# A new order for the first 740 steps of a hand-ordered retention and SwiGLU kernel, and one more warm-up product

## The chip, the cores and the metric

The kernel runs on one core of a Trainium2 chip. The metric is the device time of one execution in microseconds (us). The core has a matrix engine (TensorE, in the profile PE, its weight loads PEld), three engines for elementwise work (VectorE or DVE, ScalarE or ACT, GpSimd or POOL), and SyncE (SP), whose queue issues nearly all transfers (DMA). Every engine runs its own instructions strictly in program order, and engines meet through semaphores. "On a queue" below always means in such an order.

## The reference

Two blocks in a row. The first is a recurrent retention over 4 batches, 8 heads, 768 positions, head size 64; the second a SwiGLU feed-forward block over the 3072 tokens with model size 512 and hidden size 1536.

```python
for t in range(S):
    state = gamma[None, :, None, None] * state + np.einsum('bhd,bhe->bhde', k[:, :, t], v[:, :, t])
    y[:, :, t] = scale * np.einsum('bhd,bhde->bhe', q[:, :, t], state)
...
x = np.ascontiguousarray(attn_out.transpose(0, 2, 1, 3)).reshape(B * S, H * D)
...
g = x @ w_gate
silu = g * (1.0 / (1.0 + np.exp(-g)))
val = x @ w_val
return (silu * val @ w_out).astype(np.float32)
```

The three weight matrices arrive in double precision and are converted in the kernel.

## The kernel before, in words

The tokens are cut into four segments. A segment is six chunks of 128 positions: three positions in each of two batches. For a chunk, retention is computed in blocks: scores (keys times queries, masked by a decay), their product with the values, the product of the queries with the carried state, and the update of the state. Then the segment goes through the feed-forward block: 12 blocks f of 128 hidden columns, gate and value products ("up"), the gating, and the product with w_out ("down") into six PSUM banks, one for each token block.

Matrix products work on fp32r operands. To keep accuracy, an operand is split into three parts (near_a and far_a on ACT, near_b and far_b on DVE, near_c or far_c on POOL or DVE) and a product is the sum over three parts. In the first segment the weights are loaded in double precision, converted by steps a, b, S, c, C on ACT, DVE and POOL, combined by T, split by n, used, and written to DRAM (Z) for the later segments.

There is no scheduler at run time. The order is written out by hand in the string PLAN: 2372 names of steps, and run() (in tile_retnet_swiglu) issues each step's instructions in that order. An instruction goes to the queue of its engine, so the plan fixes the order on each of the five queues at once; between engines only the semaphores of real dependencies hold. The same steps in another order compute the same values. The steps that the text names are these (f, n, p are numbers; a prefix such as 1/ is the segment, and none is the first part of segment 0):

- lN:W loads chunk N (W 0 keys, 1 queries, 2 values, 3 keys by rows); A0, A1, A2 load the table of decays; U, V load raw weights, Z keeps converted ones; P0, P1, P2 and 1/lN load chunks for segment 1; L loads two small vectors; all are issued by SP.
- rN transposes the keys of a chunk (lines 686), sN makes scores (646), mN mixes with the values (744), oN adds the old state (722), tN updates the state (707); kN and qN scale values and queries on POOL (663, 659), EN copies the rows.
- p, v are the up products of f = 0, 1 in three column parts (1080), G and W the gate and value products of f = 2 to 11 (1062), two each; i and u are SiLU on ACT, j and y the multiplication on DVE; g scales the state; h2 is a small preparation of tables for segment 1, M0 and M1 load its mask.
- 0/Wf loads a block of w_out into one of three split buffers, 0/df.0, .1, .2 split it, 0/Zf writes the split form to DRAM (so that 0/W of a later block waits until the 0/Z that reads the same buffer has landed); 0/hf.0, .1, .2 split the hidden values; 0/Df.b is the down product of block f for token block b (1306).
- 1/scp, 1/Ap, 1/Bp, 1/Cp are the matrix steps of segment 1's retention for p = 0, 1, 2 (830): scores, and three parts of the mixing. They need 1/decp (mask, DVE), 1/qp (scaled queries), 1/kp.i (scaled keys, mostly eight small ACT instructions each, line 973), 1/was (decayed state, ACT, 1031) and 1/new (added state, DVE, 1037). 1/y copies results out, 1/sum and 1/x build the operands of segment 1's up products, 1/p (1235), whose weights come by 1/Lf and 1/wf.

Before the plan starts, warm_up issues products of a zeroed tile with itself, ten of 128 columns and five of 16, on TensorE (line 1425; a product in this number format is two passes).

Of the kernel before, what the change touches and what calls it, by code (L numbers as in the profile page):

```python
# [25 lines left out]
L = 3  # L26
# [49 lines left out]
    1/y0.03 1/y0.05 0/d2.1 0/D1.5 1/y0.00 0/W3 0/D1.3 0/h2.1 1/y0.07 1/y0.12 1/y0.14 1/y0.13 1/l4  # L76
# [19 lines left out]
    1/w0.1.0 0/D11.4 1/sum2.2 0/Z11 1/x2.0.0 1/w0.0.2 1/w1.0.0 1/x2.1.1 1/x2.0.1 0/Z10 1/w1.0.1 0/e0
    0/o0 1/x2.0.2 1/w1.0.2 0/D11.5 1/p0.0 1/u0.0 1/p0.1 1/p0.2 1/p1.0 1/x2.2.0 1/u0.1 1/w0.2.0 0/e2
    0/o2 1/x2.2.1 1/w0.1.1 1/p1.1 1/w1.1.0 1/x2.2.2 1/u0.3 1/w1.2.0 1/u1.0 1/p1.2 1/u0.2 1/w0.2.1
    1/L3 1/w0.1.2 1/w1.2.1 1/w0.2.2 0/e1 1/p0.3 1/w2.2.0 1/w2.1.0 1/u0.4 0/e3 1/w1.1.1 1/w1.1.2 1/L4
    1/p0.4 1/u1.1 1/u0.5 1/p0.5 2/ta 1/w2.0.0 1/u0.6 1/u1.3 1/p0.6 1/p1.3 1/u1.4 1/u0.8 1/p1.4  # L100
# [18 lines left out]
    1/w10.0.2 1/p9.3 1/p9.2 1/u9.4 1/p8.6 1/u9.3 1/p9.4 1/p9.5 1/u8.2 1/u8.8 1/u8.9 1/p10.0 1/u9.5
    2/sc0 1/w9.2.2 1/u9.6 1/u9.1 1/p10.1 2/l5 2/l6 1/u8.7 1/w11.1.0 1/w11.0.0 1/w11.0.1 1/w11.1.1  # L120
    1/u10.0 1/w11.2.0 1/p10.2 1/p9.6 1/W0 2/l2 2/k0.1 1/u10.3 1/p10.3 1/u9.8 1/u9.9 1/p10.4 1/u10.4
    1/p10.5 1/h0.0 1/u10.1 2/dec0.0 1/u7.7 1/u9.2 1/u10.2 1/w10.2.1 1/u10.5 1/w11.1.2 1/w11.0.2
# [196 lines left out]
T0, UP0 = 30.0, 8.35  # L319
# [1188 lines left out]
```

## Time and profile before

| | us |
|---|---|
| timed runs | 637.96, 642.05, 643.54 |
| median of the three | 642.05 |
| the profiled execution | 638.92 |
| its span, first to last instruction | 637.1 |
| TensorE busy | 629.8 (99%) |
| VectorE busy | 509.1 (80%) |
| ScalarE busy | 394.9 (62%) |
| GpSimd busy | 178.2 (28%) |

The page divides the span into 40 slices and gives each engine's busy share in tenths; TensorE's row begins with an 8, ends with a 7, and has a 9 everywhere between. The chain that ended last is 94% TensorE and 3% DMA. TensorE's ends are modelled and its matrix products overlap in a pipeline, so that a product's mean duration in a row is longer than its distance to the next; distances are read from the chain of waits, which has no overlap. "Issue" is time in which an engine waited for nothing that the profile shows. A timeline row reads: start, duration, engine, line, operation, output and inputs, shape, count, and in brackets the idle time before it with what ended it. The granted clock of TensorE was 1.00 throughout.

### The profile page before, as it was taken

The page shows a single profiled execution, that of the slowest core. Times are in us where ns is not written, and L with a number is a line of the kernel's source. Part 1 is how long each engine was busy: PE and PEld are TensorE (multiplying, and loading weights), DVE is VectorE, ACT ScalarE, POOL GpSimd, SP SyncE. Part 2 cuts the span into 40 slices and gives each one's busy share as a digit, 9 for nine tenths or more (in the row PEclk, how much of TensorE's full clock was granted, in tenths as well). Part 3 has the DMA queues.
Part 4 walks back from the last instruction along what each step waited for, and adds up shares of the span by engine and source line. Part 5 has one row for each costly group of instructions (what it writes and reads, how often), then busy time and mean ns, then how long its engine had stood idle before and what let it go on. Part 6 is the DMA issues. An engine that isn't in the chain of part 4 may idle for free.

```text
span 637.1 us, 14140 instructions
## 1 busy us (share of the span) xinstructions
PE 629.8 (99%) x5607; PEld 581.2 (91%) x5607; DVE 509.1 (80%) x773; ACT 394.9 (62%) x836; POOL 178.2 (28%) x120
## 2 busy tenths in 40 slices
PE   8999999999999999999999999999999999999997
PEld 7999999978779999998788999998788999999886
DVE  6997898988989889977789677978878888877551
ACT  3787888677667665667477565656864655564220
POOL 3625555523532541120001343240002024232000
PEclk9999999999999999999999999999999999999999
DMA  8899998788876443687883436477785235303664
GB/s 314 280 350 345 344 359 291 289 309 309 295 268 232 162 164 119 191 272 222 276 320 120 155 109 223 158 228 217 237 303 198 102 135 190 133 17 133 231 214 149
DMA packets 58514, 142.82 MB, mean 224 GB/s; under 512 B 6864, under 2 KB 29264, under 8 KB 58448
## 3 DMA queue, kind: packets, MB, share of 16 engines
q1 hardware_dynamic: 57872, 141.14, 64.8%
q8 instruction: 44, 0.72, 0.5%
q10 hardware_dynamic: 576, 0.79, 0.3%
q14 instruction: 22, 0.18, 0.1%
HBM read 112.02 MB, written 29.88 MB: 223 GB/s over the span
## 4 chain that ended last, share of the span: by engine, by line
PE 94%; DMA 3%; DVE 1%; POOL 1%; issue 0%; ACT 0%; SPq 0%; DVEq 0%; POOLq 0%
PE bank L1235 41%; PE bank L1306 29%; PE bank L1062 13%; PE bank L830 5%; PE bank L1080 3%; DMA loads<-wup 1%; DMA hT<-in_q_t_dram 1%; DMA oitem<-wdnt 1%; PE bank L646 1%; DMA hT<-in_k_t_dram 1%; PE bank L744 1%; PE bank L722 1%; PE bank L707 0%; POOL gitem L1140 0%; POOL hT L659 0%
## 5 line engine op out<-in xcount | busy, mean ns | idle before, releaser
L1306 PE MATMUL bank<-oitem,gitem 128*128 128x512 f32 (+1 forms) x873 | 204.2, 391 | 0.5 <-DMA oitem<-wdnt 0.5
L1306 PEld LDWEIGHTS bank<-oitem,gitem 128*128 128x128 f32 x873 | 160.9, 188 | 34.8 <-DMA oitem<-wdnt 1.2
L1235 PE MATMUL bank<-xa,gitem 128*128 128x384 f32 x864 | 160.9, 335 | 0.0
L1235 PEld LDWEIGHTS bank<-xa,gitem 128*128 128x128 f32 x864 | 150.6, 188 | 0.4 <-DVE xa L1150 0.2
L1140 POOL TENSOR_TENSOR gitem<-gitem 128x768 fp32r<-128x768 f32 x36 | 72.4, 2014 | 185.0 <-DVE gitem L1137 160.2
L1140 POOL TENSOR_TENSOR oitem<-oitem 128x512 fp32r<-128x512 f32 (+1 forms) x48 | 53.6, 1124 | 157.6 <-DVE oitem L1137 125.7
L411 DVE SCALAR_TENSOR_TENSOR gitem<-gitem 128x768 fp32r<-128x768 f32 x84 | 86.0, 1033 | 1.3
L1235 PE MATMUL bank<-xb,gitem 128*128 128x384 f32 x432 | 84.0, 335 | 0.4 <-POOL gitem L1140 0.4
L1062 PE MATMUL bank<-xa,oitem 128*128 128x384 f32 x480 | 84.2, 335 | 0.0
L1062 PEld LDWEIGHTS bank<-xa,oitem 128*128 128x128 f32 x480 | 83.0, 188 | 0.3
L1235 PEld LDWEIGHTS bank<-xb,gitem 128*128 128x128 f32 x432 | 75.8, 188 | 1.1 <-POOL gitem L1140 0.7
L1134 ACT ACTIVATE gitem<-loads 128x768 fp32r<-128x768 f32 x72 | 59.1, 842 | 24.8 <-PE bank L1235 15.4
L1137 DVE SCALAR_TENSOR_TENSOR gitem<-gitem,loads 128x768 fp32r<-128x768 f32 x72 | 70.6, 993 | 3.4 <-ACT gitem L1134 3.3
L1134 ACT ACTIVATE gitem<-hT 128x768 fp32r<-128x768 f32 x48 | 40.1, 844 | 43.6 <-PE bank L1306 34.1
L1137 DVE SCALAR_TENSOR_TENSOR gitem<-gitem,hT 128x768 fp32r<-128x768 f32 x48 | 46.5, 978 | 22.5 <-ACT gitem L1134 18.6
L1235 PE MATMUL bank<-xb,oitem 128*128 128x384 f32 x216 | 43.0, 335 | 0.0
L1235 PEld LDWEIGHTS bank<-xb,oitem 128*128 128x128 f32 x216 | 38.0, 188 | 0.0
L1251 ACT COPY tmp<-bank 128x384 f32<-128x384 f32 x36 | 17.2, 479 | 27.0 <-PE bank L1235 20.8
L1252 DVE TENSOR_TENSOR hT<-bank,tmp 128x384 f32<-128x384 f32 x36 | 20.0, 555 | 16.3 <-PE bank L1235 16.2
L1250 ACT COPY tmp<-bank 128x384 f32<-128x384 f32 x36 | 17.2, 478 | 24.5 <-PE bank L1235 16.9
L1254 DVE TENSOR_TENSOR hT<-hT,bank 128x384 f32<-128x384 f32 x36 | 19.7, 550 | 13.4 <-ACT bank L1254 13.2
L1137 DVE SCALAR_TENSOR_TENSOR oitem<-oitem,loads 128x256 fp32r<-128x256 f32 (+1 forms) x42 | 24.6, 588 | 3.7 <-ACT oitem L1134 3.6
(157 smaller groups left out, 806.0 us busy)
## 6 DMA issues: line engine op xcount, KB each, us to landing
loads<-wup SPq DMA_DIRECT2D x36, 896.0 KB, 5.1
oitem<-wdnt SPq DMA_DIRECT2D x33, 768.0 KB, 4.9
wdnt<-oitem SPq DMA_DIRECT2D x12, 768.0 KB, 5.8
wup<-first SPq DMA_DIRECT2D x9, 896.0 KB, 7.1
rawp<-in_w_gate_dram SPq DMA_DIRECT2D x12, 512.0 KB, 7.3
rawp<-in_w_val_dram SPq DMA_DIRECT2D x12, 512.0 KB, 6.6
rawp<-in_w_out_dram SPq DMA_DIRECT2D x12, 512.0 KB, 6.4
out_dram<-chunk_x SPq DMA_DIRECT2D x21, 256.0 KB, 4.4
```

Source lines behind the costliest of these rows:

```text
L411: stt(o, x, 1.0, y, op0=mul, op1=op)
L830: nc.tensor.matmul(o, a, b, start=start, stop=True, skip_group_check=True)
L1062: nc.tensor.matmul(o, w[:, a, ts(b, P)], X0[:, a, i, NC - 1 - b], start=a == b == 0, stop=a == 2 and b == NC - 1, skip_group_check=True)
L1080: nc.tensor.matmul(o, w[:, a, ts(b, P)], X0[:, a, :, NC - 1 - b, ts(j, P)], start=a == b == 0, stop=a == 2 and b == NC - 1, skip_group_che ...
L1134: act(o[0], x, AF.Copy, scale=CUT / FAR)
L1137: stt(o[1], f32(o[0]), -FAR, x, op0=mul, op1=add)
L1140: op(o[2], f32(o[0]), f32(o[1]), op=add)
L1235: nc.tensor.matmul(o, w[:, a, k], x[:, a, KH - 1 - k], start=start and a == k == 0, stop=a == 2 and k == KH - 1, skip_group_check=True)
L1250: steps = (lambda: copy(p1, x), lambda: tt(c11, z, p1, op=add), lambda: act(gate, c11, AF.Silu, scale=ONE), lambda: copy(u2, x), lambda: c ...
L1252: lambda: copy(p5, wb), lambda: tt(h1, x, p5, op=add),
L1254: lambda: act(x, x, AF.Silu, scale=ONE), lambda: tt(h1, h1, x, op=mul))
L1306: nc.tensor.matmul(o, hs[g][:, a, ds(i * TH + u * P, P)], wo[g][:, a, cols], start=n == 0 and (f == 0 or final), stop=f == NF - 1 and a == ...
```

## The change

The 2372 steps are the same in both plans. From step 740 on, the order is the same; of the 740 before, nearly all stand at another place. Orders within a kind mostly stay (the order in which split buffers, score banks and parts p are taken does). Among what moves:

- At the start l0:0 goes ahead of A0, and A2 behind l0:2; m0 goes ahead of r1; U1:1 stays behind l4, l5:1 moves up; V0:0 goes ahead of l3:0 and l2:2 ahead of l3:1; k2 goes ahead of q3.
- P0 moves from step 137 to 391, L from 111 to 153, l4:3 from 174 to 310, P2 from 378 to 283, l5:3 from 285 to 139.
- Many of the G and W products swap within their pair; G6:0 goes ahead of W5:0 and W5:1; t4 and t5 move back among the f = 9 and 10 products.
- 1/A0, 1/B0 and later 1/A1, 1/B1, 1/C1, 1/A2, 1/B2, 1/C2 move ahead relative to the 0/D products, the 0/D products of a block change their order, and 1/k, 1/q, 1/was, 0/h and 0/d on the other engines move with them.
- On SP, Z9, Z10 and Z17 move back, 1/l4, 1/l8 and 1/l10 forward, 1/l11 and 1/l9 back, 0/Z2 ahead of 1/l7, 0/W4 and 1/l6.

The other edit is the count of warm-up products. The core of the diff, with the lines that hold the steps named in this document:

```diff
 PLAN = """
-    A0 l0:0 A2 l1:0 l0:2 l1:2 U0:0 k0 A1 I2 r0 I1 l2:1 I0 l2:0 s0 r1 l3:1 l2:2 K0 s1 a0:1 k1 b0:1 m0
-    J0 S0:1 m1 q2 l3:0 V0:0 t0 c0:1 E1 J1 x0:1 l3:2 C0:1 l2:3 s2 t1 q3 l4:1 x1:1 l4:0 k2 o2 U1:1
...
-    p0:2 P0 a12 n2:0 T0:1 u1:1 T0:2 S3 U4:3 n2:1 u0:2 c3 v0:2 y1:1 Z0 p1:2 v1:2 C3 T1:0 n2:3 U13:1
...
-    S6 i4:1 T5:0 j4:0 c6 Z4 W4:1 C6 b7 S7 T5:1 T5:2 U14:3 G5:0 n6:0 G5:1 c7 j4:1 n6:3 n6:1 n5:5 W5:0
-    i5:0 n6:4 W5:1 C7 i5:1 a8 C13 b8 j5:0 n6:2 n6:5 n7:0 S8 j5:1 n7:1 G6:0 U9:1 c14 Z13 G6:1 Z5 l5:3
...
-    W8:0 i8:0 C15 C10 t4 U16:3 n9:4 T8:1 W8:1 j8:0 T9:0 Z15 i8:1 0/h0.0 n9:2 G9:0 T9:1 c16 t5 n9:5
...
-    Z16 a17 W10:0 T11:0 0/h0.1 T11:1 Z9 j10:0 T11:2 1/sc0 n11:1 W10:1 b17 n11:2 c17 G11:0 T10:1 Z11
...
-    1/was0.0 0/d0.1 j11:0 i11:1 1/k0.0 W11:1 0/d0.2 1/dec0.1 0/D0.0 1/q0.1 0/D0.1 0/D0.2 j11:1
-    0/h4.0 0/W1 1/q0.0 Z10 1/k0.1 0/d1.0 Z17 0/D0.4 0/h4.1 0/h1.1 0/W2 1/A0 0/Z0 0/h1.2 0/D0.5
-    1/y0.06 1/l11 0/D0.3 1/new0.0 0/d1.1 1/y0.01 1/B0 0/h3.0 0/d2.0 0/d1.2 0/h3.1 0/D1.2 1/y0.04
...
-    0/D1.4 0/h2.2 0/Z1 1/y0.15 0/d2.2 1/y0.02 1/C0 1/was0.1 1/y0.16 0/d3.0 0/D1.0 0/h3.2 1/l7
-    1/y0.17 1/new0.1 1/y0.11 1/sum0.0 0/D1.1 0/D2.3 0/D2.1 1/begin 0/W4 0/h4.2 1/x0.2.0 1/y0.10
-    0/h5.0 0/D2.2 0/d3.1 0/d3.2 0/D2.0 1/x0.2.2 1/was1.0 1/l6 1/sum0.2 1/x0.2.1 1/sc1 0/Z2 0/h5.1
-    0/D2.4 1/q1.1 0/D3.0 0/d4.0 0/D2.5 0/Z3 0/D3.4 1/dec1.0 0/W5 0/d4.1 0/D3.2 0/D3.1 0/D3.3
-    1/dec1.1 1/x0.1.0 0/d4.2 1/sum0.1 1/k1.1 0/h6.0 1/k1.0 1/sum0.3 0/Z4 0/d5.0 0/D3.5 0/d5.1 0/W6
-    0/h5.2 0/D4.4 1/x0.0.0 0/D4.2 1/q1.0 1/x0.1.1 1/l9 0/h6.1 1/x0.1.2 0/d5.2 0/D4.5 0/Z5 1/A1
...
-    0/D7.4 1/q2.1 1/x1.1.1 0/d8.1 0/D7.3 0/d8.2 1/x1.1.2 0/h11.0 0/D8.0 0/h9.2 1/x1.2.2 0/d9.0
-    0/D8.2 0/d9.1 1/was2.0 1/q2.0 1/l10 0/W10 0/D8.4 0/Z8 1/sum1.3 1/k2.1 0/d9.2 0/h11.1 0/D8.3
-    0/D8.1 0/d10.0 1/A2 1/x1.0.0 0/D9.4 0/d10.1 0/D8.5 0/D9.0 1/new2.0 1/y2.00 1/B2 0/h10.1 1/y2.07
...
+    l0:0 A0 l1:0 l0:2 I2 A2 r0 l1:2 U0:0 A1 I1 I0 K0 l2:1 l2:0 l2:2 k0 s0 s1 m0 k1 r1 m1 a0:1 l3:1
+    b0:1 J0 V0:0 q2 S0:1 l3:0 t0 E1 J1 c0:1 g2 x0:2 l3:2 l2:3 s2 l4:0 k2 C0:1 t1 l4:1 n0:0 x1:1 x1:2
...
+    j4:1 n6:2 a8 G6:0 C7 W5:0 n6:4 W5:1 T5:2 T6:0 T6:1 b8 T6:2 U9:1 i5:1 n6:5 G6:1 n7:0 n7:3 Z5 P2
...
+    S11 c11 G9:1 i9:1 n10:0 T9:0 G9:0 t4 n10:1 Z8 n9:5 i9:0 n10:2 n10:3 T9:1 a16 C11 W9:1 t5 G10:0
+    W9:0 b16 P0 U17:2 i10:0 G10:1 n11:0 T9:2 n10:4 n10:5 n11:3 j9:1 0/h1.0 S16 j9:0 n11:4 C16 T11:0
+    W10:0 Z16 T11:1 T11:2 i10:1 n11:1 0/h0.1 n11:2 a17 b17 0/h0.2 c17 Z11 W10:1 1/sc0 j10:0 n11:5
...
+    1/dec0.0 i11:0 Z9 1/k0.0 C17 j11:0 1/k0.1 1/dec0.1 T10:1 W11:1 1/l4 1/q0.0 T10:2 1/A0 0/d0.2
+    j11:1 0/d1.0 1/y0.06 1/new0.0 0/D0.5 0/W2 0/D0.3 1/y0.01 0/D0.1 1/B0 0/h2.0 0/D0.2 0/h4.0 0/h1.2
+    0/Z0 1/y0.13 0/h2.1 1/y0.03 1/y0.14 0/h4.1 0/D0.4 0/d1.1 0/d2.0 0/d1.2 0/D0.0 1/y0.15 1/y0.05
...
+    0/D2.5 0/D2.1 1/y0.12 1/y0.16 1/x0.2.0 0/Z1 1/new0.1 1/y0.11 0/Z2 1/y0.10 0/h5.0 1/sum0.0
+    1/x0.1.0 0/D2.4 0/d3.2 1/sum0.1 1/sum0.3 0/D2.0 1/was1.0 1/x0.1.2 0/h5.1 0/D2.3 1/sc1 1/l7
+    0/D3.5 0/D3.4 0/W4 0/h6.0 0/D3.2 1/sum0.2 1/l6 0/W5 0/h5.2 1/q1.1 1/x0.0.0 1/dec1.0 0/d4.0
+    1/x0.2.2 0/D3.3 0/Z3 1/l8 0/D3.1 1/x0.2.1 0/d4.1 1/dec1.1 1/k1.0 1/k1.1 0/D3.0 1/q1.0 0/d4.2
+    1/A1 0/W6 0/D4.3 1/x0.1.1 0/d5.0 0/h6.1 0/D4.1 1/y1.00 1/y1.06 1/new1.0 0/d5.1 1/y1.07 1/y1.01
...
+    1/l10 0/W8 1/y1.10 0/D6.1 1/x1.2.2 0/h9.0 0/D6.2 1/sc2 0/Z6 1/was2.0 1/sum1.2 0/d8.0 1/dec2.0
+    0/D7.5 0/D6.4 0/D7.1 1/q2.1 0/D7.0 1/sum1.0 1/x1.1.0 1/dec2.1 1/k2.1 0/h9.1 1/sum1.1 1/q2.0
+    0/D7.2 0/h10.0 0/d8.1 0/d8.2 0/Z7 0/D7.4 1/x1.1.2 1/sum1.3 1/A2 0/D7.3 1/x1.1.1 0/W9 0/h11.0
...
-    warm_up(10)
+    warm_up(11)
```

More of the change, by code (lines that the diff above doesn't have):

```diff
@@ L96 @@
[L96 to L100, printed above, removed]
@@ L119 @@
[L119 to L122, printed above, removed]
-    1/p11.0 1/u11.0 2/td 2/dec0.1 1/w10.2.2 1/p10.6 1/u10.8 1/u10.6 1/h0.1 1/w11.2.1 1/u10.7 1/h0.2
-    1/w11.2.2 2/l11 2/l10 1/p11.2 1/p11.1 1/p11.3 1/u11.3 1/p11.4 2/cv0 1/u11.4 1/h1.0 1/p11.5
@@ new lines @@
+    2/x0.0.1 2/y1.01 1/h8.0 1/h8.1 1/D5.0 1/D5.3 1/D5.1 1/D5.4 2/was1.10 2/q2.1 2/mv1.0 1/D6.1 2/B1
+    2/y1.10 2/y1.11 2/x1.1.0 2/q2.0 1/h7.1 1/h7.2 2/new1.1 1/D6.5 1/D6.3 2/l13 2/k2.3 1/h9.0 2/k2.1
+    2/mv1.1 1/D6.4 1/D6.2 2/x1.2.0 2/k2.0 1/D6.0 1/h10.0 1/h9.1 1/h8.2 1/W7 1/D7.2 1/D7.1 1/D7.3
+    1/D7.5 1/W8 1/D7.4 1/D8.4 2/k2.2 2/A2 2/was2.00 2/x0.0.2 2/sum1.0 2/sum1.1 2/sum1.2 2/sum1.3
+    2/L2 2/L1 1/W9 2/L0 1/D8.3 2/was2.01 1/h9.2 2/x1.1.1 2/x1.1.2 2/x1.2.2 2/x1.0.0 2/new2.0 1/D8.2
+    1/D7.0 1/h11.0 1/D8.5 1/D8.0 1/D8.1 2/x1.2.1 2/mv2.0 2/y2.00 2/y2.01 2/B2 2/y2.10 2/y2.11
@@ new lines @@
+    2/x2.1.0 1/h10.1 1/h11.1 2/x1.0.2 1/h11.2 2/x1.0.1 2/sum2.2 2/x2.1.2 2/sum2.0 2/sum2.1 1/h10.2
+    2/w0.0.0 2/was2.10 2/x2.1.1 2/w0.0.1 1/D9.3 1/D9.0 1/D9.1 1/D9.4 1/D9.5 1/D9.2 1/W10 1/W11
+    2/w0.2.0 1/D10.0 1/D10.3 2/sum2.3 2/w0.2.1 2/w0.2.2 2/was2.11 2/x2.0.0 2/x2.2.0 2/new2.1
+    2/w0.1.0 2/x2.2.2 2/x2.0.1 2/w0.1.1 2/x2.2.1 1/D10.4 1/D10.1 1/D10.5 1/D10.2 2/w1.0.0 1/D11.0
+    1/e0 1/D11.1 1/D11.4 1/D11.3 1/D11.2 1/D11.5 2/L3 2/w0.0.2 2/p0.0 2/x2.0.2 1/e1 2/p0.1 1/o1
+    2/w0.1.2 2/p0.3 1/e2 2/w1.2.0 2/w1.2.1 2/w1.0.1 2/u0.0 2/u0.1 2/p0.2 2/w2.2.0 2/w1.1.0 2/w1.1.1
@@ new lines @@
+    2/D8.2 2/D8.1 2/h10.1 3/x1.0.2 3/new2.0 2/h10.2 3/mv2.0 2/D8.5 2/D8.0 3/L0 2/h11.0 3/w0.0.0
+    2/h11.1 3/w0.0.1 3/w0.0.2 3/y2.01 3/x1.0.1 2/W9 2/D9.5 2/D9.1 2/D9.3 2/D9.2 2/D9.0 2/D9.4
+    3/w0.1.0 3/w0.1.1 2/W10 2/W11 3/w0.2.0 3/w0.2.1 3/L3 3/B2 3/y2.10 2/h11.2 3/y2.11 3/x2.2.0
+    3/sum2.0 3/sum2.1 3/w0.1.2 3/sum2.3 3/x2.1.0 2/D10.5 2/D10.4 2/D10.0 2/D10.2 2/D10.3 2/D10.1
+    3/w1.2.0 2/D11.0 3/w1.0.0 2/D11.3 2/D11.1 3/x2.1.2 3/x2.1.1 3/p0.0 2/D11.4 2/D11.5 2/D11.2
+    3/sum2.2 3/x2.2.2 3/w1.0.1 3/x2.2.1 2/e0 3/p0.1 3/x2.0.0 3/x2.0.2 3/x2.0.1 3/u0.0 3/p0.2
@@ new lines @@
+    3/D4.4 3/D4.5 3/D4.2 3/D4.1 3/D4.3 3/D4.0 3/W7 3/h7.0 3/h5.1 3/h5.2 3/D5.4 3/D5.1 3/D5.2 3/D5.3
+    3/h7.1 3/h7.2 3/h6.1 3/h8.0 3/u10.9 3/h8.1 3/h6.2 3/D6.3 3/D5.0 3/D6.0 3/D5.5 3/h9.0 3/D6.2
+    3/D6.4 3/D6.1 3/D6.5 3/D7.2 3/D7.4 3/D7.5 3/D7.0 3/D7.3 3/D7.1 3/u11.8 3/h8.2 3/u11.9 3/h10.0
+    3/h11.0 3/W8 2/o4 3/D8.2 3/D8.4 3/D8.1 3/D8.5 3/D8.3 3/D8.0 3/h9.1 3/h9.2 3/W9 3/h11.1 3/h10.1
+    3/h10.2 3/h11.2 3/W10 3/W11 3/D9.0 3/D9.3 3/early 3/D9.1 3/D9.4 3/D9.5 3/D10.4 3/D10.5 3/D11.4
+    3/D11.5 3/e4 3/o4 3/e5 3/o5 3/D10.0 3/D11.0 3/e0 3/o0 3/D10.3 3/D11.3 3/e3 3/o3 3/D10.1 3/D11.1
```

281 lines of the change are left out of this document (135 added, 146 removed).

## The prediction

> **What bounds the kernel now.** I read the page's head, then the busy time by stretch, then TensorE's waits, and for single places the timeline and the chain of waits.
>
> ```profile
> span 637.1 us, 14140 instructions
> ```
>
> ```profile
> 0.00:12.30 12.30, 10.50 (x118) 9.21 (x118) 6.61 (x19) 3.84 (x7) 3.55 (x8) 1.00 0.85 296
> 12.30:130.00 117.70, 117.69 (x960) 114.92 (x961) 104.47 (x153) 93.92 (x155) 60.34 (x39) 1.00 0.93 324
> 130.00:140.00 10.00, 8.58 (x170) 6.73 (x169) 8.95 (x11) 6.42 (x20) 3.38 (x2) 1.00 0.90 324
> 140.00:200.00 60.00, 59.63 (x746) 48.21 (x745) 51.18 (x75) 43.08 (x117) 21.62 (x13) 1.00 0.77 281
> ```
>
> The columns after the length are busy time of PE, PEld, DVE, ACT and POOL, then the granted clock, the DMA share and GB/s. TensorE is the bound: from 12.30 to 130.00 it is busy for 117.69 of 117.70 us at full clock. The reordered steps fill the span to about 200 us, and nearly all of what they could still save is listed here:
>
> ```profile
> PE bank L830 <- issue: 1.4, 1, 1.4
> PE bank L1425 <- DVE warm L1440: 1.1, 1, 1.1
> PE bank L1306 <- DMA oitem<-wdnt: 0.5, 1, 0.5
> PE bank L646 <- POOL hT L659: 0.5, 1, 0.5
> PE bank L1235 <- POOL gitem L1140: 0.4, 1, 0.4
> ```
>
> Five waits, 3.9 us in all. The 1.1 is before the first warm-up product and the 0.5 for oitem<-wdnt lies behind the reordered steps (wdnt is read back from the second segment on), so 1.4 + 0.5 + 0.4 = 2.3 us is all that the profiled execution could give up. This execution took 638.92 us: 637.10 of span and 1.82 around it. The three timed runs are 637.96, 642.05 and 643.54; their median lies 3.1 us above the profiled time. Those 3 to 5 us are in no row: the profile shows one of the quick executions.
>
> **The change, part by part: the start.**
>
> ```profile
> 5.25 5.60 DMA hT<-in_q_t_dram
> ...
> 10.98 1.28 POOL hT L659
> ...
> 12.31 1.16 PE bank L646 x16
> ```
>
> ```profile
> 1.08 4.19 PE L1425 MATMUL bank<-warm 128*128 128x128 f32 x30 [1.08 <-DVE warm L1440]
> ```
>
> In the chain of waits TensorE's full stretch begins at 12.31 with scores s2, released by POOL's scaling q2 of a chunk that l2:1 loads (5.60 us). Moved on SP's queue: l0:0 goes ahead of A0, A2 behind l0:2; the set of loads ahead of l2:1 is the same (A0, A2, l0:0, l1:0, l0:2, l1:2, U0:0, A1), as are POOL's steps ahead of q2 (k0, k1) and TensorE's ahead of s2 (r0, r1, s0, s1, m0, m1, t0 in another order). So s2 stays at 12.3: 0, bounded by -0.5 (the whole wait for POOL, were q2 early) and +0.5 (the same again). The eleventh warm-up product is two more passes; thirty took 4.19 us, 0.14 each, so 0.28 us at the head of TensorE's queue, with r0 behind it. The 0.5 us wait at s2 covers it; uncovered it costs 0.28. Taken: 0.
>
> **From s2 to the first D products, 12.3 to 130.** Idle there is 0.01 us, so nothing can be gained. The up products G and W swap places within pairs, except that G6:0 goes two products ahead and t4, t5 two to three back.
>
> ```profile
> 119.97 10.23 PE bank L1062 x59
> ```
>
> Twelve passes of 10.23/59 = 0.173 us make a product of 2.08 us, so G6:0 comes 4.2 us earlier, behind its weight split n6 (ACT, DVE, POOL). Those steps move ahead as well, and POOL is busy for only 60.34 of 117.70 us. Loss between 0 and 4.2; I take 0.3, since every other product moves by one place at most. On SP, P0 (512 KB) leaves the place after U12 and goes ahead of U17, where its only reader, 1/sc0, is still some 10 us off; at 324 GB/s that frees 1.6 us of a queue whose share is 0.93. l4:3 moves back in the same way. Both help only transfers that already land in time: 0.
>
> **The first mixing steps, 130 to 140.**
>
> ```profile
> 130.20 2.76 PE bank L1306 x12
> ```
>
> ```profile
> 121.59 1.52 DVE L411 SCALAR_TENSOR_TENSOR first<-first 128x256 f32<-128x256 f32 x1
> 130.01 0.83 ACT L1134 ACTIVATE gitem<-hT 128x768 fp32r<-128x768 f32 x1
> 130.75 2.01 ACT L973 ACTIVATE loads<-loads,local 128x64 f32<-128x64 f32 x8
> 130.78 0.68 DVE L411 SCALAR_TENSOR_TENSOR loads<-loads,tab 128x512 f32<-128x512 f32 x1
> 132.89 0.70 PE L830 MATMUL bank<-tmp,loads 64*64 64x64 f32 x32
> 133.64 0.66 PE L830 MATMUL bank<-loads 64*64 64x64 f32 x32
> 136.58 0.40 PE L830 MATMUL bank<-loads,states 64*64 64x64 f32 x13
> 138.40 0.33 PE L830 MATMUL bank<-loads,states 64*64 64x64 f32 x3 [1.42 <-issue]
> ```
>
> A D product is three passes of 0.23, 0.69 us. The new order runs 1/A0 straight behind W11:1, ahead of the four D products that preceded it: it is reached at 132.89 - 2.76 = 130.13. It needs q0.0, and from its last part on (the second x32, 0.75 later) k0.1. On DVE the 1.52 of T10:2 goes behind q0.0, which so ends at 131.46 - 1.52 = 129.94, in time. On ACT two splits of 0.83 (h2.0, h4.0) go behind k0.1, which ends at 132.76 - 1.66 = 131.10 against 130.88: 0.2 us of waiting, bounded by 0 and by 1.9 (were k0.1 not earlier at all).
>
> The 1.42 us is the largest item. It falls inside one step, 1/B0, after 13 of 16 passes whose like had just run, and nothing is named as releaser. The page's instruction queue offers a cause:
>
> ```profile
> q8 instruction: 44, 0.72, 0.5%
> ```
>
> 0.72 MB in 44 packets is 16 KB a packet, fetched beside data queues at a share of 0.90. 1/A0 and 1/B0 are the densest instruction bursts there, and only two D products lay between them. In the new order there are three, and four D products no longer precede 1/A0, so the burst meets its fetch 0.69 us later at least. Bounds: -1.42 (gone) and 0 (the same wait elsewhere); I take -1.2, for a wait that depends on such a phase seldom returns whole. [...]
>
> **The second and third mixing steps, 140 to 200.**
>
> ```profile
> 148.58 0.64 ACT L1143 ACTIVATE oitem<-oitem 128x512 fp32r<-128x512 f32 x1 [1.84 <-issue]
> 152.30 2.01 ACT L973 ACTIVATE loads<-loads,local 128x64 f32<-128x64 f32 x8
> 155.61 0.69 PE L830 MATMUL bank<-tab,loads 64*64 64x64 f32 x32
> 155.88 1.04 ACT L1143 ACTIVATE xa<-tmp 128x1024 fp32r<-128x1024 f32 x1
> ```
>
> Three D products fewer precede 1/A1 (24 for 27): 155.61 - 2.07 = 153.54, and 152.34 with the 1.2 regained. ACT's new order before it is h6.0, x0.0.0, d4.0, k1.0, k1.1. d4.0 (148.58) waits for the load W4; h6.0 and x0.0.0 (0.83 + 1.04) fit its idle 1.84, and k1.1 ends at 148.58 + 0.64 + 2 x 2.01 = 153.24. It is needed 0.75 us into 1/A1, at 153.09: a wait of 0.2. If W4 lands behind the 768 KB that now precede it (2.4 us at 324 GB/s) the wait is 2.6. Taken: 0.3.
>
> ```profile
> 174.82 0.85 ACT L1134 ACTIVATE gitem<-hT 128x768 fp32r<-128x768 f32 x1 [4.55 <-PE bank L1306]
> 176.09 1.27 ACT L1031 ACTIVATE states<-states,local 128x128 f32<-128x128 f32 x4
> 177.27 2.01 ACT L973 ACTIVATE tmp<-tmp,local 128x64 f32<-128x64 f32 x8
> 178.57 0.69 PE L830 MATMUL bank<-tmp,loads 64*64 64x64 f32 x32
> ```
>
> Six D products fewer precede 1/A2 (4.1 us: 174.4). But was2.0 and k2.1, which stood behind h11.0 and its 4.55 us of idle, now stand ahead of h10.0, so 1.27 + 2.01 us of work run in that idle and end some 4.5 us earlier: 0, bounded by 1.3 us (one was2.0 late).
>
> ```profile
> 196.81 2.70 POOL gitem L1140
> ```
>
> The last wait, 0.4 us at 1/p1.0, hangs on this POOL step and the DVE steps before it, whose order is the old one; with mixing done earlier DVE arrives earlier, but TensorE too: -0.2, between -0.4 and +0.8.
>
> The sum: 0 + 0.3 + 0.2 - 1.2 + 0.3 + 0 - 0.2 = -0.6 us, 638.3 for an execution like the profiled one. For the median I start from the mean of the four executions shown, (637.96 + 638.92 + 642.05 + 643.54)/4 = 640.6, and forecast **640.0 us**.
>
> **Rivals.** *Late executions mend.* The 3 to 5 us of the two long executions may be data waits in the reordered steps; loads that move ahead (l2:2, V0:0, 1/l4, 1/l8, 1/l10) would end them. For it: a DMA share of 0.93. Against: the profile holds no such wait. Time: 638.92 - 1.42 - 0.4 = 637.1. [...] *SP's queue jams at 0/Z2*:
>
> ```profile
> 140.16 0.68 DVE L1150 SCALAR_TENSOR_TENSOR oitem<-oitem 128x512 fp32r<-128x512 f32 x1
> 142.66 0.33 SPq L940 DMA_DIRECT2D loads<-in_k_n_dram  x1
> 146.44 1.06 SPq L1294 DMA_DIRECT2D wdnt<-oitem  x2
> ```
>
> 0/Z2 waits for d2.2 (ended 140.84). It stood behind 1/l7 (142.66), W4 and 1/l6; now it stands ahead of all three, which bring k1, D4 and 1/A1 their data. It decides when d2.2 ends after 142.66. With transfers 4.6 us late (643.54 against 638.92) it ends at 145.4: 1/l7 is 2.8 us late and lies behind Z2's 2.4 us, so 5.2 us more at 1/A1: 643.54 + 5.2 = 648.7. Against it: in the profiled execution the slack is 1.8 us.
>
> **Numbers.** Forecast 50% (638 to 642), late executions mend 24%, the wait stays 14%, the jam 12%, in which two parts in three come out over 1%. About 1% (6.4 us) is what a measurement of this kernel can tell from no change. Under 635.6 could come only from the first rival's lower end: 5%. Over 648.5 the jam: 8%, and 1% for anything unseen. The range runs from 636.0 (the first rival less about 1) to 646.0 (a jam at half price), leaving some 5% below and 11% above.
>
> **What would show it.** Right: s2 at 12.3; no wait between 12.3 and 130; no issue wait in 1/B0; under 1 us at 1/A1. Wrong: any single TensorE wait over 2 us before 200, a wait for oitem ahead of D4, or an issue wait of a microsecond at another dense step. The forecast fails if the median leaves 636 to 646, or if quick executions differ from 638.3 by over 2 us.

## The result, and the profile after

| | before | changed |
|---|---|---|
| median of 20 timed runs (us) | 642.62 | 639.33 |
| lowest, highest | 637.96, 645.86 | 637.77, 642.76 |
| runs above 643 us | 9 | 0 |
| profiled execution | 638.92 | 639.04 |
| its span | 637.1 | 637.3 |

The ratio of changed to before is 0.9957, with a 95% interval from 0.9936 to 0.9977: 0.4% faster, well inside the 1% that the prediction called no change. The medians lie 3.3 us apart, the lowest runs 0.2 us, and the two profiled executions are equally long. What the change took away is not in the profile of before: it is the long executions.

TensorE's waits in the profile of the changed kernel:

```profile
PE bank L1425 <- DVE warm L1440: 1.1, 1, 1.1
PE bank L830 <- ACT chunk_x L1169: 0.6, 1, 0.6
PE bank L646 <- POOL hT L659: 0.3, 1, 0.3
```

The issue wait of 1.4 us, the 0.4 us for gitem and the 0.5 us for oitem<-wdnt are gone; a wait of 0.6 us for the copy of the mixing results (chunk_x, the steps 1/y) is new. 3.9 us of waits have become 2.0, and the span is no shorter. The busy time by stretch, with the columns as in the prediction:

```profile
0.00:12.30 12.30, 11.08 (x112) 9.96 (x114) 5.97 (x17) 3.33 (x5) 2.83 (x7) 1.00 0.83 284
12.30:130.00 117.70, 117.38 (x971) 114.38 (x966) 103.70 (x153) 92.44 (x152) 60.17 (x40) 1.00 0.91 314
130.00:140.00 10.00, 10.00 (x174) 8.19 (x173) 8.20 (x13) 8.64 (x28) 3.08 (x2) 1.00 0.99 388
140.00:200.00 60.00, 59.30 (x742) 47.98 (x741) 55.37 (x75) 41.26 (x113) 19.61 (x14) 1.00 0.83 289
```

In 130 to 140 TensorE is now busy throughout and the transfers' share has risen from 0.90 to 0.99. "Busy" hides the rest. The timeline from 10 to 15 us and at 130 (start, duration, engine, line, what; in brackets the idle time before it):

```profile
11.71 1.28 POOL L659 TENSOR_TENSOR hT<-hT,tab 128x512 f32<-128x512 f32 x1 [2.42 <-DMA hT<-in_q_t_dram]
...
13.04 1.16 PE L646 MATMUL bank<-hT 64*128 64x128 f32 x16 [0.32 <-POOL hT L659]
...
129.85 3.20 ACT L973 ACTIVATE loads<-loads,local 128x64 f32<-128x64 f32 x13
130.98 0.70 PE L830 MATMUL bank<-tmp,loads 64*64 64x64 f32 x32
131.50 0.41 PE L830 MATMUL bank<-loads,states 64*64 64x64 f32 x16
131.73 1.70 PE L830 MATMUL bank<-loads 64*64 64x64 f32 x32
```

s2 starts at 13.04 and not at 12.31, since l2:1 landed 0.7 us later. And 1/A0 is slower without a single wait being listed: its last 32 passes took 1.70 us where the same 32 took 0.66 before. They read what 1/k0.1 scales, the last eight of these short ACT instructions, which end at 129.85 + 3.20 = 133.05; TensorE follows them piece by piece, no pass beginning more than 0.13 us after the one before it, and each piece of idle time is too short for the list. 1/A0 costs 1.04 us more that way. In all six profiles whose computing has the new order here, these passes end 0.36 to 0.38 us behind 1/k0.1. What made 1/k0.1 late is the load of the keys. ACT stood idle for it before the first of the sixteen instructions of 1/k0.0 and 1/k0.1; in the kernel before it began them at 128.08 without such a wait:

```profile
129.12 3.93 ACT L973 ACTIVATE loads<-loads,local 128x64 f32<-128x64 f32 x16 [1.70 <-DMA loads<-in_k_n_dram]
```

Added up over the reordered steps, by the distance from each step of TensorE to the next: s2 +0.73, 1/A0 +1.04, 1/B0 -1.73 (its 2.83 us are 1.09 now), 1/B1 +0.70 for the wait ahead of it and +0.28 inside it, 1/sc2 +0.39, the wait at 1/p1.0 -0.66. The sum is +0.75. Seen at the step after 1/p1.0 (the third row of before, the second of after), it is 201.74 - 201.04 = +0.70:

```profile
198.30 0.88 PE L1235 MATMUL bank<-xb,gitem 128*128 128x384 f32 x4
199.55 1.66 PE L1235 MATMUL bank<-xb,gitem 128*128 128x384 f32 x8 [0.36 <-POOL gitem L1140]
201.04 2.24 PE L1235 MATMUL bank<-xa,gitem 128*128 128x384 f32 x12
```

```profile
199.66 2.24 PE L1235 MATMUL bank<-xb,gitem 128*128 128x384 f32 x12
201.74 1.55 PE L1235 MATMUL bank<-xa,gitem 128*128 128x384 f32 x8
```

So this execution of the changed kernel was 0.7 us behind at 200 us. It gets most of that back at 304, where the kernel before waits for a block that it reads back (the 0.5 us for oitem<-wdnt) and the changed one arrives after the block has landed.

### The profile page after: what moved, and what is told of

Read it like the earlier page. It is cut to its first block, busy times and chain, and to the rows that moved or that the text cites. A ratio compares the mean times of both kernels' runs of the same rounds, so it can differ in the third digit from the quotient of the medians.

```text
span 637.3 us, 14162 instructions
## 1 busy us (share of the span) xinstructions
PE 631.7 (99%) x5609; PEld 583.2 (92%) x5609; DVE 511.0 (80%) x773; ACT 394.2 (62%) x836; POOL 174.7 (27%) x120
## 4 chain that ended last, share of the span: by engine, by line
PE 96%; DMA 3%; SPq 0%; POOL 0%; issue 0%; DVE 0%; ACT 0%; POOLq 0%
PE bank L1235 41%; PE bank L1306 30%; PE bank L1062 13%; PE bank L830 6%; PE bank L1080 3%; DMA hT<-in_q_t_dram 2%; DMA loads<-in_q_t_dram 1%; PE bank L646 1%; PE bank L722 1%; PE bank L744 1%; PE bank L707 0%; DMA oitem<-wdn 0%; POOL hT L659 0%; SPq L603 0%; DVE chunk_x L1332 0%
## 5 line engine op out<-in xcount | busy, mean ns | idle before, releaser
L1137 DVE SCALAR_TENSOR_TENSOR gitem<-gitem,hT 128x768 fp32r<-128x768 f32 x48 | 47.8, 1002 | 23.0 <-ACT gitem L1134 19.1
L1251 ACT COPY tmp<-bank 128x384 f32<-128x384 f32 x36 | 17.2, 479 | 27.0 <-PE bank L1235 20.8
L1250 ACT COPY tmp<-bank 128x384 f32<-128x384 f32 x36 | 17.2, 478 | 24.9 <-PE bank L1235 17.1
L1252 ACT COPY tmp<-bank 128x384 f32<-128x384 f32 x36 | 17.3, 479 | 16.5 <-PE bank L1235 11.7
```

The costliest lines, as they stand in the source:

```text
L1137: stt(o[1], f32(o[0]), -FAR, x, op0=mul, op1=add)
L1250: steps = (lambda: copy(p1, x), lambda: tt(c11, z, p1, op=add), lambda: act(gate, c11, AF.Silu, scale=ONE), lambda: copy(u2, x), lambda: c ...
L1252: lambda: copy(p5, wb), lambda: tt(h1, x, p5, op=add),
```

## The experiments

Every run below was timed beside the kernel before on the same chip; a ratio is to that. 440 is the number of the step 12 ahead of the first down product, at about 125 us. Kernels that mix the two orders keep each order's own sequence within its part; their diffs below state the PLAN as a rule, where the kernel has it written out, and they have ten warm-up products, as every kernel below but the two made from the changed one further down.

**Where does the gain lie?** The kernel before once more, the new order without the eleventh product, and the two halves of the reordering apart.

> The kernel before, unchanged, timed against itself and profiled once more. Two theories are tried in this set. Theory L (late executions): the change leaves a quick execution where it was (638 to 639 us) and takes its 3.3 us of median from the long executions, in which transfers land late and TensorE waits. Theory B (the wait at 1/B0): the gain is the 1.42 us wait of the profiled execution, gone in every execution, and the rest is chance. Both expect a ratio to itself between 0.998 and 1.002, a median near 642.6 and a spread from 638 to 646. Should the profile catch an execution above 641 us, L expects single TensorE waits on transfers (or on a step that follows one) that add up to its excess over 638.9; B expects the 1.4 us wait at 1/B0 and no new one. If such an execution shows no waits and longer distances between products, both fall.

```diff
-    warm_up(11)
+    warm_up(10)
```

> The new order with ten warm-up products as before: only the eleventh product is undone. My term for it was 0 to 0.28 us. Theories L and B both expect the time of the changed kernel, 639.3 (639.0 to 639.7). If the eleventh product matters beyond that, as a shift of everything behind it, the median leaves 638.5 to 640.2.

```diff
-PLAN = old
+PLAN = sorted(old[:440], key=place_in_new) + old[440:]
```

> The first 440 steps of the plan of before (start, weight conversion, up products G and W, down to 12 steps ahead of the first down product), put among themselves in the new order; everything after them in the old order; ten warm-up products. L, if the late transfers are those of the weight conversion or the start (12 to 130 us): 639.5. L, if they are those of the mixing steps: 642.6. B: 642.6, with the 1.4 us wait still at 1/B0.

```diff
-PLAN = old
+PLAN = old[:440] + sorted(old[440:], key=place_in_new)
```

> The counterpart: the first 440 steps in the old order, the 300 behind them in the new one; ten warm-up products. L with late transfers in the first 130 us: 642.6. L with late transfers in the mixing steps: 639.5. B: 641.2 (642.6 less 1.42), with no issue wait at 1/B0 in the profile.

| | ratio, 95% interval | median | highest | above 643 us |
|---|---|---|---|---|
| before beside them (35) | 1 | 640.03 | 646.41 | 8 |
| before again (12) | 0.9994 (0.9954 to 1.0033) | 641.22 | 646.89 | 4 |
| new order, ten products (12) | 0.9958 (0.9929 to 0.9986) | 637.86 | 639.50 | 0 |
| new first 440 (12) | 1.0046 (1.0012 to 1.0079) | 643.61 | 646.82 | 8 |
| new from 440 (12) | 0.9969 (0.9940 to 0.9997) | 639.31 | 642.48 | 0 |

The gain that shows lies behind step 440, and the eleventh product has no part in it that shows. How much of it the steps from 440 make alone is loose: by the plain means their kernel is at 0.9983 of before (639.47 against 640.57 us), inside the interval of the table but nearer to 1 than its 0.9969. The first 440 steps in the new order make the old rest slower: P0 and Z9 now go out in the crowded stretch from 107 to 132, and 0/W2 lands at 138.0 instead of 134.2. Theory B is half refuted: the kernel with the new steps from 440 is 1.1 us faster in the mean than before, but the wait at 1/B0 isn't why, as the second profile of the kernel before shows:

```profile
137.41 0.40 PE L830 MATMUL bank<-loads,states 64*64 64x64 f32 x13
138.34 0.33 PE L830 MATMUL bank<-loads,states 64*64 64x64 f32 x3 [0.53 <-issue]
```

It stands behind the same 13 passes, but is 0.53 us and not 1.42, and that execution took 639.33 us, no less than the first. It had reached the place 0.8 us later and left it at the same time. In the new first 440, whose order is the old one at this place, the wait is absent, and that kernel is the slowest of the five.

**One transfer, or late transfers in general?** In the profile of the new first 440, TensorE loses 2.9 us at D5.1 and 1/B1. The chain there: 0/W5 lands late, 0/d5 and, behind it on ACT, 1/y1.00 are late, then 1/new1.0. The expectation below stops there. But what releases 1/B1 (163.61) are the copies 1/y1.07 and 1/y1.01 (163.30), which stand on ACT behind 0/d6.0 (162.65), and that waited 2.29 us for 0/W6.

```diff
-    0/h3.2 1/l7
+    0/h3.2 0/Z2 1/l7
...
-    1/sc1 0/Z2 0/h5.1
+    1/sc1 0/h5.1
```

> The plan of before with one step moved: 0/Z2 ahead of 1/l7, as in the new order. The runs so far put the gain into the steps from 440 on, and in the profile of the run with the new first 440 steps the late chain is 0/W5, 0/d5, 1/y1.00 on ACT behind it, 1/new1.0, 1/B1 (2.9 us lost at D5.3 and 1/B1). 0/W5 uses the buffer of 0/W2, free only when 0/Z2 has landed. Theory Z: the gain is 0/Z2, issued 5.6 us earlier in the new order; this kernel then takes nearly all of it, a ratio of 0.996 to 0.997, with 0/W5 landing 2 us earlier in the profile. Theory Q (the queue as a whole: 1/l11, Z10, Z17 and others moved out of the crowded stretch from 127 to 140): a ratio of 0.999 to 1.001. My forecast's rival (0/Z2 ahead of 1/l7, 0/W4 and 1/l6 jams the queue when d2.2 is late): above 1.002.

```diff
-    0/Z1 1/new0.1 1/y0.11 0/Z2 1/y0.10
+    0/Z1 1/new0.1 1/y0.11 1/y0.10
...
-    1/sum0.2 1/l6 0/W5
+    1/sum0.2 1/l6 0/Z2 0/W5
```

> The changed kernel with 0/Z2 moved back behind 1/l6, its place in the old order; everything else as changed. Theory Z: the gain is given back, a ratio to before near 1.000 (0.998 to 1.003), with a wait at D5 or 1/B1 of over 1.5 us in the profile. Theory Q: the time stays that of the changed kernel, a ratio of 0.995 to 0.997.

The kernel before with the early 0/Z2 has a ratio of 0.9999 (0.9974 to 1.0023); the changed kernel with the late one 0.9965 (0.9944 to 0.9987), a median of 638.44 and nothing above 639.63. Theory Z falls on both sides. So does the prediction's rival: ahead of 1/l7, 0/W4 and 1/l6 the step 0/Z2 jams nothing, because d2.2 ended at 140.85 in the changed kernel, as at 140.84 before.

In the next two kernels the first write of the split weights goes out twice; `again`, the tile that takes the second copy, is declared beside wdnt.

```diff
-            at(t + z, f"{s}/Z{f}", lambda: nc.sync.dma_start(out=w_dn3[f], in_=wo[f].bitcast(U32)))
+            at(t + z, f"{s}/Z{f}", lambda: [nc.sync.dma_start(out=d, in_=wo[f].bitcast(U32)) for d in ([again, w_dn3[f]] if f == 0 else [w_dn3[f]])])
```

> The kernel before with the write 0/Z0 done twice (the second copy, 768 KB, goes to a place that nothing reads): transfers behind it are made late on purpose, by about 2.4 us at 324 GB/s, and 0/W3, which waits for that buffer, with them. Theory L (the old order is sensitive to late transfers in the mixing steps, and that is where its long executions come from): 2 to 4 us slower than before, a ratio of 1.003 to 1.007, with waits at 0/D3 to 0/D5 or 1/B1. If late transfers there cost nothing, 0.999 to 1.001, and the long executions come from elsewhere.

> The changed kernel with the same write done twice. Theory L with an order that bears late transfers: at most 1 us slower than the changed kernel, a ratio to before of 0.995 to 0.998. If both orders are equally sensitive: 2 to 4 us slower than the changed kernel, a ratio of 0.999 to 1.003.

The kernel before with the doubled write has a ratio of 1.0041 (1.0015 to 1.0067), the changed one 1.0003 (0.9985 to 1.0021). Against its own 0.9957 that is 0.46% lost, about as much as the old order loses (0.41%): by this measure the two orders are equally sensitive, and my expectation that the new one bears late transfers better failed. But the profile of the first one caught an execution of 646.12 us, and shows what a long one can be made of. Its waits, and its busy time by stretch around the place:

```profile
PE bank L1306 <- DMA oitem<-wdnt: 1.9, 2, 1.4
PE bank L830 <- ACT chunk_x L1169: 1.5, 1, 1.5
PE bank L1425 <- DVE warm L1440: 1.1, 1, 1.1
PE bank L1306 <- POOL oitem L1146: 1.0, 2, 0.8
PE bank L1306 <- DVE oitem L1150: 0.4, 2, 0.2
```

```profile
152.80:160.00 7.20, 6.78 (x101) 4.63 (x99) 4.99 (x8) 5.52 (x18) 1.09 (x2) 1.00 0.99 378
160.00:163.40 3.40, 1.74 (x6) 0.86 (x5) 2.58 (x5) 0.91 (x4) 0.78 (x1) 1.00 0.96 345
163.40:170.20 6.80, 5.96 (x73) 4.88 (x73) 5.16 (x5) 5.60 (x15) 2.74 (x3) 0.50 0.82 286
170.20:180.00 9.80, 9.80 (x147) 7.86 (x146) 7.37 (x13) 4.88 (x12) 3.28 (x3) 1.00 0.57 198
```

The last three columns are the granted clock, the DMA share and GB/s. From 160.0 to 163.4 TensorE is busy for 1.74 of 3.40 us. Then its granted clock is 0.50 for 6.8 us, and its products take nearly twice as long (0.43 us from pass to pass, below): the waits at this place come to 3.2 us by the distances between steps, and 5.96 us of work at half speed are some 3.0 us more, by estimate. TensorE's own rows show both:

```profile
160.84 0.50 PE L1306 MATMUL bank<-oitem,gitem 128*128 128x512 f32 x1 [0.82 <-POOL oitem L1146]
161.56 1.21 PE L1306 MATMUL bank<-oitem,gitem 128*128 128x512 f32 x4 [0.23 <-DVE oitem L1150]
164.24 0.88 PE L830 MATMUL bank<-loads,states 64*64 64x64 f32 x13 [1.47 <-ACT chunk_x L1169]
...
166.44 4.06 PE L1306 MATMUL bank<-oitem,gitem 128*128 128x512 f32 x9
```

Nine passes in 4.06 us, where nine took 2.34 in the kernel before: from pass to pass it is 0.43 us instead of 0.23. At the step behind them (170.43, before 163.92) this execution is 6.5 us behind the first profile, of 6.9 at its end (spans of 644.0 and 637.1). And ACT's rows show why 1/B1 (164.24) waited; the second fence has the same steps in the kernel before:

```profile
151.41 0.63 ACT L1143 ACTIVATE oitem<-oitem 128x512 fp32r<-128x512 f32 x1 [4.18 <-DMA oitem<-wdn]
...
158.80 0.63 ACT L1143 ACTIVATE oitem<-oitem 128x512 fp32r<-128x512 f32 x1 [1.68 <-DMA oitem<-wdn]
159.34 1.04 ACT L1143 ACTIVATE xa<-tmp 128x1024 fp32r<-128x1024 f32 x1
160.29 0.52 ACT L1169 COPY chunk_x<-bank 64x128 f32<-64x128 f32 x2
163.28 0.63 ACT L1143 ACTIVATE oitem<-oitem 128x512 fp32r<-128x512 f32 x1 [2.47 <-DMA oitem<-wdn]
163.93 0.55 ACT L1169 COPY chunk_x<-bank 64x128 f32<-64x128 f32 x2
```

```profile
155.34 0.63 ACT L1143 ACTIVATE oitem<-oitem 128x512 fp32r<-128x512 f32 x1 [1.04 <-issue]
155.88 1.04 ACT L1143 ACTIVATE xa<-tmp 128x1024 fp32r<-128x1024 f32 x1
157.06 0.54 ACT L1169 COPY chunk_x<-bank 64x128 f32<-64x128 f32 x2
158.26 0.63 ACT L1143 ACTIVATE oitem<-oitem 128x512 fp32r<-128x512 f32 x1 [0.66 <-DMA oitem<-wdn]
159.63 0.55 ACT L1169 COPY chunk_x<-bank 64x128 f32<-64x128 f32 x2 [0.73 <-DVE states L1037]
```

The three oitem rows are d4.0, d5.0 and d6.0, which wait in ACT's queue for 0/W4, 0/W5 and 0/W6. The copies 1/y1.00 and 1/y1.06, ready at about 157.5 by TensorE's end of 1/A1, stand behind d5.0 until 160.29, and 1/new1.0, on DVE behind the last split of block 5, ends at 163.04. What comes last are the copies 1/y1.07 and 1/y1.01 (163.93): they stand behind d6.0, and the chain of waits leads from there over 0/W6 (157.70 to 163.17) to the write 0/Z3 (152.04 to 157.65), which reads the buffer that 0/W6 fills. In the first profile d6.0 ended at 158.89, ahead of 1/new1.0 (159.59), and cost nothing.

This is a place where the new order differs: the old plan has "0/d6.0 1/y1.07 1/y1.01" and then 1/B1, the new one has 0/d6.0 behind 1/B1, so that a late 0/W6 can't hold 1/B1 there. No run moved 0/d6.0 alone.

What made the clock fall, these rows don't say. The gaps ahead of the fall were 0.82 us, 0.23 us and the first 0.6 us of the 1.47, three of them in 3.40 us, with TensorE busy for half of that time. That it was busy for only half is not enough as a cause: in a later profile (of the kernel before with 1/l11 moved, below) TensorE was busy for less of a stretch of that length, 1.57 of 3.41 us, with one gap of 2.01 us, and kept its clock:

```profile
445.39:448.80 3.41, 1.57 (x108) 1.44 (x100) 1.29 (x2) 3.35 (x12) 0.00 (x0) 1.00 0.63 138
```

So what decides is not found here.

**The clock of the timed executions.** A record of the granted clock is kept for each timed execution of these runs (not for the first 20 of before). Its mean is 1.000 or 0.999 in most and 0.997 or less in others; 0.003 of 640 us is 1.9 us, or 3.8 us at half clock (the 0.50 of the profile above).

| kernel | executions | with a clock of 0.997 or less | their median | median of the others |
|---|---|---|---|---|
| before, beside all experiments | 104 | 28 | 642.8 | 639.4 |
| before again | 12 | 6 | 644.1 | 638.8 |
| changed | 20 | 0 | | 639.3 |
| new order, ten products | 12 | 0 | | 637.9 |
| new from 440 | 12 | 0 | | 639.3 |
| changed, 0/Z2 late | 12 | 0 | | 638.4 |
| changed, 0/Z0 twice | 12 | 2 | 642.2 | 640.3 |
| before, 0/Z0 twice | 12 | 6 | 643.1 | 641.5 |
| before, 0/Z2 early | 12 | 1 | 644.7 | 639.0 |
| new first 440 | 12 | 8 | 643.7 | 642.5 |

The clock falls in 34 of 116 executions of the kernel before and in none of 56 in the four kernels with the new order behind step 440. Where it stays up, the medians of the two orders lie within about 1 us of each other. In the runs beside the first two sets, leaving out the executions with a lowered clock takes the mean of before from 640.57 to 639.61 and from 640.44 to 639.48: 0.96 us each, where the three shorter experiments with the new order gained 2.6, 1.1 and 1.9 us on the mean. So the executions with a lowered clock make 0.96 us of gains of 1.1 to 2.6, about half. The rest lies in executions whose clock stayed up (5 of those 76 of before are above 643). None of these was profiled, and that they hold longer waits is only argued. The nearest is the profile with 1/l11 moved, of 641.49 us at a clock of 1.00: TensorE waits 2.9 us in all for blocks that are read back (oitem<-wdnt), 2.01 us of it at 448.98, behind the reordered steps. An execution can thus also be long where the two plans are the same. In the first comparison the mean of before was 642.41 us, 1.4 to 2.9 us above those of the later sets; how often its clock fell is not known, so this part of the 3.3 us can't be divided.

**Transfers or computing?** Steps behind 440 with one of the two taken from the new order and the other from the old. SP's sequence in the old order and in the new one (the first kernel below has the new one, with the other engines in the old order; the second the reverse):

```diff
-    0/W1 Z10 Z17 0/W2 0/Z0 1/l11 0/W3 1/l4 0/Z1 1/l7 0/W4 1/l6 0/Z2 0/Z3 0/W5 0/Z4 0/W6 1/l9
+    0/W1 1/l4 0/W2 0/Z0 Z10 Z17 0/W3 0/Z1 0/Z2 1/l7 0/W4 1/l6 0/W5 0/Z3 1/l8 0/W6 0/Z4 1/l11
```

> First 440 steps old; behind them all steps of the four computing engines in the old order and only SP's transfers in the new one (1/l4, 0/Z2, 0/W5 and 1/l8 earlier, 1/l11, 1/l9 and 0/Z3 later); ten warm-up products. With old transfers and old computing the ratio is 1, with both new (e4) it was 0.9969. Theory Q (the transfers' order makes the gain): 0.995 to 0.998, executions above 643 gone. Theory P (TensorE's order makes it: the new one keeps five products of block 4 back until 1/A1 is through and runs the first product of block 5 behind 1/C1 instead of ahead of 1/B1, so that late 0/W5 and 0/d5 find TensorE busy): 0.999 to 1.002, executions above 643 as often as before (one in six), and TensorE still waiting between D5.3 and 1/B1 in the profile.

> The counterpart: first 440 steps old, behind them the four computing engines in the new order and SP's transfers in the old one; ten warm-up products. Theory P: 0.995 to 0.998, no execution above 643, and a first product of block 5 that waits for nothing. Theory Q: 0.999 to 1.003, with waits of over 1 us for block 4's or 5's operands in the profile. If both parts are needed, this and e9 both lie between 0.998 and 1.000.

In both, the exchange runs on past step 740, nearly to the end of the plan: in segment 2 a load goes ahead of the products of block 0, which then use the weights of block 2. That part of the result is changed, and TensorE stands still for 5 us there, so the ratios of 1.0184 and 1.0326 say nothing about the question. The profiles do, up to 200 us. With the new transfers alone, TensorE's wait between D5.3 and 1/B1 is gone. With the new computing alone, this is the timeline's first long wait, and these are the stretches around it and around 1/A2:

```profile
160.28 0.88 PE L830 MATMUL bank<-loads,states 64*64 64x64 f32 x13 [3.09 <-ACT chunk_x L1169]
```

```profile
155.00:159.40 4.40, 2.19 (x9) 1.46 (x9) 0.90 (x2) 1.00 (x3) 0.32 (x1) 1.00 0.85 294
159.40:163.00 3.60, 2.72 (x65) 2.58 (x66) 3.60 (x5) 0.94 (x5) 0.94 (x1) 0.61 0.53 184
177.00:183.50 6.50, 2.65 (x13) 1.81 (x11) 6.50 (x10) 0.92 (x2) 0.95 (x1) 1.00 0.79 271
183.50:187.00 3.50, 3.33 (x81) 3.05 (x82) 1.30 (x4) 0.50 (x1) 0.00 (x0) 0.59 0.02 5
```

Twice TensorE is busy for less than half of a stretch, with a single gap of 3.09 us in the first and of 3.55 us in the second, and twice its clock falls after it. The new computing order needs the new order of the transfers; theory P, by which TensorE's order alone makes the gain, falls.

The same question with the exchange ended at step 740, and the most suspect single transfer alone:

> The question of e9 again, with the exchange of the transfers' order ended at step 740, so that the later segments are those of before: steps 441 to 740 with SP's transfers in the new order, all computing in the old one. In e9's profile TensorE lost 0.3 us between the end of 1/C0 and 1/sc1's successors up to 1/sc2, where the profiles of the old transfers lost 0.3 to 7.4. Theory Q (the transfers' order makes the gain): a ratio of 0.995 to 0.998, and no execution above 643 of 12. If new transfers gain only with the new computing order: 0.999 to 1.002.

```diff
-    1/y0.06 1/l11 0/D0.3
+    1/y0.06 0/D0.3
...
-    0/d5.1 0/W6
+    0/d5.1 0/W6 1/l11
```

> The plan of before with one step moved: 1/l11 (a load for the third mixing step, issued at 131.6 between 0/Z0 and 0/W3) behind 0/W6, as late as the new order has it. If this one load, in the stretch where Z10, Z17, 0/W2 and 0/Z0 are all under way, is what makes 0/W4 and 0/W5 late, the ratio is 0.995 to 0.998 and no execution of 12 is above 643. If the gain needs more than one transfer's place: 0.999 to 1.001, executions above 643 one in six.

The new transfers alone have a ratio of 0.9979 (0.9953 to 1.0006), a median of 639.54 beside 640.82, no execution above 643, and one of 12 with a lowered clock. That is theory Q's value, but the interval doesn't exclude 1. In its profile 1/B1 waits for nothing; a wait of 1.04 us for copies stands at 1/B2. 1/l11 alone has 1.0014 (0.9983 to 1.0046), 7 of 12 with a lowered clock: it isn't this load.

**What stays open.** Which of the moved transfers matter was not found; two were tried alone, and neither makes the gain (that the clock fell in only 1 of 12 executions with the early 0/Z2 may be chance, beside 34 of 116). Whether 0/d6.0 behind 1/B1 would be enough was not tried. No long execution of the kernel before itself was profiled: that its clock falls between 155 and 170 is concluded from the kernel with 0/Z0 twice, and from the gain's place behind step 440.

## Why the prediction was right, and where it was not

The time was right (640.0 forecast, 639.33 measured, range 636.0 to 646.0) and so was the likeliest class, within 1%. The reason was not the one I gave the most weight, and that 640.0 came out so near is luck (see the median, below).

- **The start.** "s2 stays at 12.3" was too firm, and its bounds of 0.5 too narrow: s2 began at 13.04. In the other profiles it lies anywhere from 12.14 to 13.67, in both orders, though the same loads stand ahead of l2:1. Where s2 waits for POOL's scaling, and the first 440 steps are the old ones, that scaling began between 10.98 and 11.85. So the landing of l2:1 (10.85 in the kernel before, 11.58 in the changed one) was not fixed here by what is queued ahead of it.
- **The eleventh product.** 0 was right: 0.9958 without it, 0.9957 with it.
- **From s2 to 130.** +0.3 forecast; of the 0.32 us that TensorE lost in that stretch, all is the wait at s2. G6:0 two products earlier costs nothing.
- **1/A0.** +0.2 forecast with a bound of 1.9; it cost 1.04. The forecast had 1/k0.1 end at 131.10, counting only ACT's own work; it ended at 133.05, because ACT first waited 1.70 us for the load of the keys, which I hadn't looked at. TensorE then consumed the eight pieces as fast as ACT made them.
- **1/B0.** -1.2 forecast (1.2 of the 1.42 was my estimate), -1.73 measured, but it brought nothing: what was saved there was spent at s2, 1/A0 and 1/B1. The traces agree with an instruction fetch as the cause, but no run moved it alone. In the eight profiles with the old order of TensorE here, a 16 KB packet of the instruction queue q8 began between 135.28 and 136.72, and the fourteenth of the last 16 passes of 1/B0 never began less than 2.29 us after it. Five of them have the wait (0.53 to 1.42 us), and in these the pass began 2.29 to 2.39 us after the packet. In the other three (new first 440, 0/Z0 twice, 1/l11 moved) TensorE came there 2.36 to 2.78 us after the packet and found nothing to wait for. The way that I thought it would end was wrong: the burst didn't come later (1/B0 began at 135.62, before at 135.83), the packet came earlier (133.59, before 136.03). Most packets of that queue came without such a wait: the profile of before lists one issue wait of TensorE and 44 packets.
- **1/A1 and 1/A2.** +0.3 and 0 forecast. 1/A1 waited for nothing; the wait came one step later, 0.70 us at 1/B1 behind the copies 1/y1, which I hadn't looked at, and 0.39 at 1/sc2, behind a load of queries that landed at 170.63.
- **The sum** of -0.6 for a quick execution came out as +0.1 (639.04 against 638.92).
- **The median.** Here a step failed. I took the mean of four executions and moved it by -0.6, that is, I let the 3 to 5 us of the long executions stay as they were. They went. It was the first rival, "late executions mend" (24%), that named what happened, but for its time I took 637.1, the quick execution without two of its waits. The right working was the quick execution, unchanged, for nearly all runs: about 639. The forecast's 640.0 lay near that only because the mean of four was already 1.4 us under the median of three.
- **The jam at 0/Z2** (12%) did not come, and the early 0/Z2 alone changed nothing.

## What to carry to other kernels

Look at the spread of the timed runs before the profile: where they lie up to 7 us above the profiled execution, the change's effect may be in executions that the profile doesn't show, and waits summed from a quick one cannot find it. Make such an execution happen, by doubling a transfer in a crowded stretch, and profile that. Late data may cost more than the wait: in one execution here three short gaps, 1.66 us within 3.40, were followed by a granted clock of 0.50 for 6.8 us, some 3.0 us more by estimate, though one longer gap of 2.01 us in another was not. And on a queue that runs in order, ask what stands behind a step that waits for a transfer: here the late load held back copies that had nothing to do with it, and TensorE with them.

## What was not expected of the hardware

- 1.66 us of idle time within 3.40 us (3.40 - 1.74), in three pieces, was followed by a granted clock of 0.50 for 6.8 us, once; 1.84 us within 3.41 (3.41 - 1.57), in one piece, left it at 1.00.
- The warm-up varies with no change of the code. The 30 passes take 4.19 us in one profile of the kernel before and 5.01 in the other, because the passes go from 0.21 to 0.11 us at different times (at 3.9 us in the first, in the second not within the twenty passes of 128 columns); 32 passes took 5.41 in the changed kernel:

```profile
1.08 5.01 PE L1425 MATMUL bank<-warm 128*128 128x128 f32 x30 [1.08 <-DVE warm L1440]
```

```profile
1.09 5.41 PE L1425 MATMUL bank<-warm 128*128 128x128 f32 x32 [1.09 <-DVE warm L1440]
```

- A step that trails its producer piece by piece (1/A0, 1.04 us) appears in no list of waits; only the distance to the next step shows it.
